# A four-layer attention block rewritten by chunks of 512 tokens, with the next key phase issued between attention steps

## The chip, the core and the metric

The kernel runs on one core of one Trainium2 chip. The metric is the device time in microseconds (us) of one execution. Engines are named as in the profile: PE (matrix engine), PEld (its weight loads), DVE (vector engine), ACT (scalar engine, which computes the exponentials), POOL (general-purpose engine), SP (the queue that issues DMA).

## The reference

A residual stream of 2048 tokens and 1024 features passes through four layers: A, B, A, B. All inputs are bf16. The same weights are used both times.

```python
def A(x, wqkv, w_phi, wo):          # linear attention, 32 heads of 32
    q, k, v = split(x @ wqkv)
    pq, pk = q @ w_phi, k @ w_phi   # per head
    phi_q = concat(softmax(pq), softmax(-pq));  phi_k = same of pk
    kv = phi_k^T v;  z = sum(phi_k)
    return (phi_q kv / (phi_q z + 1e-6)) @ wo

def B(x, wqkv, wo):                 # softmax attention, 32 heads of 32
    p = softmax(q k^T * 32**-0.5);  return (p v) @ wo

x = x + A(layernorm(x));  x = x + B(layernorm(x))   # twice
```

In layer B the exponentials are 32 heads x 2048 x 2048 numbers. ACT works on 128 rows at a time, so that is 1024 instructions of 128x1024 per layer, and 2048 in all, in both kernels.

## The kernel before

Each layer keeps everything in SBUF and runs in phases, one after the other: layer norm and projections, attention, output projection. The attention loop: one iteration holds 128 keys, 512 queries and 4 heads, so two exponentials of 128x1024.

```python
for ii, (g, qc, kc) in enumerate(iters):
    ...
    for pr in range(2):                       # two exponentials of this iteration
        e = epool.tile([P, 2 * C512], BF16, ...)
        nc.scalar.activation(out=e[:], in_=s_cur[pr][:], func=ACT.Exp)
        e_tiles.append(e)
    if ii + 1 < len(iters):                   # scores of the NEXT iteration
        s_next = [spool.tile([P, 2 * C512], F32, ...) for pr in range(2)]
        emit_scores(*iters[ii + 1], s_next)   # 4 row-tiled matmuls, 512 wide
    for j in range(4):                        # numerator of this iteration
        nc.tensor.matmul(out=num_ps[hsl, :], lhsT=v_aug[...], rhs=e_tiles[pr][...], ...)
    for j in range(4):                        # denominator of this iteration
        nc.tensor.matmul(out=den_ps[hsl, :], lhsT=ones_bf[:, 0:DH], rhs=e_tiles[pr][...], ...)
    ...                                       # (cut)
```

The softmax here doesn't subtract the row's maximum and nothing guards it: scores larger than these inputs give would overflow.

## Time and profile before

| | before |
|---|---|
| time, median of 2 runs | 3488.39 us (3488.2 to 3488.57) |
| mean granted PE clock | 0.973 |
| attention, start of the first exponential to end of the last, two layers | 938.8 + 938.9 us |
| everything else | 1606 us |
| exponentials, start to start inside attention | 0.904 to 0.917 us |

The first two lines below are from the page: busy time by engine, then the granted PE clock in tenths over 40 equal slices of the span. The page counts PE as busy while a matmul is anywhere in its pipeline, so 92% is not a peak.

```profile
PE 3190.9 (92%) x18316; PEld 1118.3 (32%) x18432; DVE 1359.2 (39%) x2009; ACT 2360.9 (68%) x2688; POOL 0.7 (0%) x6
...
PEclk9999989999999999999999988999999999999997
```

The window view sums busy time (and instruction counts) over stretches of the span. The second and fourth stretch are the two attention phases: ACT and PE are both filled, and DVE is nearly idle. The other three are everything else.

```profile
core 0: us, PE busy (x) PEld busy (x) DVE busy (x) ACT busy (x) POOL busy (x), PEclk, DMA share, GB/s
0.00:750.00 750.00, 590.57 (x2704) 258.19 (x2757) 516.81 (x848) 241.53 (x320) 0.70 (x6) 0.96 0.18 51
750.00:1688.00 938.00, 936.85 (x6136) 271.10 (x6132) 125.53 (x62) 937.88 (x1024) 0.00 (x0) 1.00 0.00 1
1688.00:2439.00 751.00, 643.91 (x2964) 279.12 (x3020) 542.35 (x875) 242.62 (x321) 0.00 (x0) 0.95 0.16 48
2439.00:3377.00 938.00, 936.83 (x6136) 271.12 (x6132) 125.53 (x62) 937.78 (x1024) 0.00 (x0) 1.00 0.00 1
3377.00:3484.00 107.00, 82.78 (x391) 38.75 (x391) 48.99 (x162) 1.07 (x2) 0.00 (x0) 0.79 0.17 59
```

The timeline lists instructions in order of start, with the duration in the second column. These are two half iterations in attention:

```profile
1000.53 0.39 PE L274 MATMUL spsn_7743<-qT,kT 32*128 32x512 bf16 x2
...
1000.85 0.39 PE L307 MATMUL num_ps<-E_7739,v_aug 128*32 128x512 bf16 x2
...
1001.02 1.29 ACT L295 ACTIVATE E_7757<-spsn_7743 128x1024 bf16<-128x1024 f32 x1
1001.08 0.38 PE L319 MATMUL den_ps<-E_7739,ones_bf 128*32 128x512 bf16 x1
...
1001.45 0.39 PE L274 MATMUL spsn_7744<-qT,kT 32*128 32x512 bf16 x2
...
1001.77 0.39 PE L307 MATMUL num_ps<-E_7741,v_aug 128*32 128x512 bf16 x2
...
1001.94 1.29 ACT L295 ACTIVATE E_7759<-spsn_7744 128x1024 bf16<-128x1024 f32 x1
```

ACT is the engine to watch: one 128x1024 exponential starts every 0.92 us (1001.02, 1001.94). It is recorded as 1.29 us long, so its record overlaps that of the next one; the first of a layer, with nothing in front of it, takes 1.02 us. So read the starts and not the durations. PE issues the scores of the next iteration (L274, `spsn`) as soon as a score tile is free, and does numerator (L307) and denominator (L319) while ACT works on the other tile. ACT never waits. Note that PE too is recorded as busy through the same 0.92 us; as these records include the pipeline, they do not show how much it could spare.

### The profile page before, as it was taken

To read this page: it belongs to the slowest core of one execution; us is meant where nothing else is said; L and a number is where in the kernel's file an instruction comes from. 1 tells how busy PE (TensorE), PEld (TensorE's weight loads), DVE (VectorE), ACT (ScalarE), POOL (GpSimd) and SP (SyncE) were. 2 spreads that over 40 slices of the span, in tenths; PEclk is the share of its full clock that TensorE was granted. 3 is DMA by queue.
4 is the path that set the end of the run, shared out by engine and by line. 5 is a ranking of instruction groups with operands and counts; after the bars stand their busy time and mean duration, and the time that the engine had idled before them with its cause. 6 is when DMAs were issued, how large, how long until landed. Compare 5 with 4: busy or idle time off the path is not lost.

```text
span 3483.5 us, 44252 instructions
## 1 busy us (share of the span) xinstructions
PE 3190.9 (92%) x18316; PEld 1118.3 (32%) x18432; DVE 1359.2 (39%) x2009; ACT 2360.9 (68%) x2688; POOL 0.7 (0%) x6
## 2 busy tenths in 40 slices
PE   2898679999999999999979976899999999999998
PEld 1343224432222222222334422344222222222223
DVE  2978876621111111111288888566011111111114
ACT  0125861039999999999312298100999999999970
POOL 0000000000000000000000000000000000000000
PEclk9999989999999999999999988999999999999997
DMA  6000001320000000000310000043000000000001
GB/s 132 15 1 1 1 25 61 128 78 1 1 1 1 1 1 1 1 1 1 74 49 1 1 1 0 25 145 121 1 1 1 1 1 1 1 1 1 1 25 49
DMA packets 112170, 82.67 MB, mean 24 GB/s; under 512 B 54624, under 2 KB 103776, under 8 KB 111968
## 3 DMA queue, kind: packets, MB, share of 16 engines
q1 hardware_dynamic: 111968, 79.84, 7.9%
q8 instruction: 144, 2.36, 0.3%
q14 instruction: 58, 0.48, 0.0%
HBM read 63.05 MB, written 4.19 MB: 19 GB/s over the span
## 4 chain that ended last, share of the span: by engine, by line
PE 75%; ACT 11%; DVE 10%; SPq 2%; issue 1%; DMA 1%; ACTq 0%; DVEq 0%
PE num_ps L307 19%; PE den_ps L319 13%; PE ps L167 7%; PE ps L222 6%; PE ps L245 3%; PE pkps L422 3%; ACT L548 2%; ACT L546 2%; DVE tmp L131 2%; ACT ebt L509 2%; DVE phik L449 1%; DVE xnT L134 1%; DVE ssum L445 1%; ACT e L441 1%; PE ps L142 1%
## 5 line engine op out<-in xcount | busy, mean ns | idle before, releaser
L330 DVE RECIPROCAL rden<-den_ps 128x512 f32<-128x512 f32 x64 | 214.9, 3358 | 1626.9 <-PE den_ps L319 1626.9
L274 PEld LDWEIGHTS <-kT 32*128 32x128 bf16 x4096 | 311.7, 91 | 872.8 <-issue 872.8
L307 PEld LDWEIGHTS <-v_aug 128*32 128x32 bf16 x4096 | 197.1, 93 | 465.6 <-issue 465.6
L222 PE MATMUL ps<-xnc,wslab 128*128 128x512 bf16 x1004 | 230.8, 386 | 15.2 <-DVE xnc L134 13.4
L167 PE MATMUL ps<-oT,wo_t 128*128 128x512 bf16 x1000 | 226.4, 386 | 16.2 <-DMA wo_t<-in_B_wo_dram 14.6
L422 PE MATMUL pkps<-W_pk,xnT 128*128 128x512 bf16 x994 | 239.2, 379 | 1.4
L441 ACT ACTIVATE e<-pkps 128x512 bf16<-128x512 f32 x128 | 76.2, 597 | 225.8 <-PE pkps L422 197.9
L117 ACT ACT_TABLE_LOAD x16 | 20.5, 1283 | 298.8 <-DVE t_386 L114 94.4
L319 PEld LDWEIGHTS <-ones_bf 128*32 128x32 bf16 x4096 | 208.8, 95 | 0.0
L491 PE MATMUL pqps<-xnT,W_pq 128*128 128x512 bf16 x496 | 160.7, 440 | 1.5 <-issue 0.7
L167 PEld LDWEIGHTS <-wo_t 128*128 128x128 bf16 x1024 | 101.7, 99 | 149.8 <-issue 33.9
L222 PEld LDWEIGHTS <-wslab 128*128 128x128 bf16 x1024 | 101.4, 99 | 142.8 <-issue 27.6
L142 PE MATMUL ps<-wv,xnT 128*128 128x512 bf16 x502 | 117.0, 380 | 21.6 <-DVE xnT L134 20.2
L174 DVE TENSOR_TENSOR xT<-xT,ps 128x512 bf16<-128x512 bf16 x128 | 87.4, 687 | 123.6 <-PE ps L167 121.7
L422 PEld LDWEIGHTS <-xnT 128*128 128x128 bf16 x1024 | 95.2, 98 | 91.6
L245 PE MATMUL ps<-wslab,xnc 128*128 128x512 bf16 x504 | 111.4, 379 | 0.4
L445 DVE TENSOR_REDUCE ssum<-e 128x16 f32<-128x512 bf16 x128 | 87.6, 685 | 39.6 <-ACT e L441 38.7
L449 DVE TENSOR_TENSOR phik<-e,rs 128x512 bf16<-128x512 bf16 x128 | 88.0, 691 | 11.8
L491 PEld LDWEIGHTS <-W_pq 128*128 128x128 bf16 x512 | 55.9, 110 | 92.0 <-issue 52.5
L546 ACT ACT_TABLE_LOAD x64 | 82.1, 1283 | 1.1
L548 ACT ACT_TABLE_LOAD x64 | 82.1, 1283 | 1.1
L509 ACT ACTIVATE ebt<-pqps 128x512 bf16<-128x512 f32 x128 | 74.5, 598 | 11.8 <-PE pqps L491 5.8
(9623 smaller groups left out, 7096.0 us busy)
## 6 DMA issues: line engine op xcount, KB each, us to landing
wslab<-in_B_wqkv_dram SPq DMA_DIRECT2D x48, 1024.0 KB, 5.0
wo_t<-in_A_wo_dram SPq DMA_DIRECT2D x2, 2048.0 KB, 9.7
wv<-in_A_wqkv_dram SPq DMA_DIRECT2D x2, 2048.0 KB, 7.9
wo_t<-in_B_wo_dram SPq DMA_DIRECT2D x2, 2048.0 KB, 8.8
out_dram<-tr SPq DMA_DIRECT2D x16, 256.0 KB, 2.0
phi<-in_A_w_phi_dram SPq DMA_DIRECT2D x64, 2.0 KB, 1.6
wqT<-in_A_wqkv_dram SPq DMA_TRANSPOSE x16, 4.2
wkT<-in_A_wqkv_dram SPq DMA_TRANSPOSE x16, 4.2
```

Source lines behind the costliest of these rows:

```text
L142: nc.tensor.matmul(ps[:], lhsT=xn_lhsT_fn(po), rhs=wv[:, po, fc * C512:(fc + 1) * C512], start=(po == 0), stop=(po == PO - 1),)
L167: nc.tensor.matmul(ps[:], lhsT=wo_t[:, po, ft * P:(ft + 1) * P], rhs=oT[:, po, cs], start=(po == 0), stop=(po == PO - 1),)
L222: nc.tensor.matmul(ps[:], lhsT=wt[:, po, gi * P:(gi + 1) * P], rhs=xnc[:, po, :], start=(po == 0), stop=(po == PO - 1),)
L245: nc.tensor.matmul(ps[:], lhsT=xnc[:, po, st * P:(st + 1) * P], rhs=wt[:, po, :], start=(po == 0), stop=(po == PO - 1),)
L274: nc.tensor.matmul(out=s_tiles[pr][:, jj * C512:(jj + 1) * C512], lhsT=kT[prt, g, k_sl], rhs=qT[prt, g, q_sl], start=True, stop=True, tile ...
L307: nc.tensor.matmul(out=num_ps[hsl, :], lhsT=v_aug[:, kc, g, j * DH:(j + 1) * DH], rhs=e_tiles[pr][:, jj * C512:(jj + 1) * C512], start=(kc ...
L319: nc.tensor.matmul(out=den_ps[hsl, :], lhsT=ones_bf[:, 0:DH], rhs=e_tiles[pr][:, jj * C512:(jj + 1) * C512], start=(kc == 0), stop=(kc == ...
L330: nc.vector.reciprocal(out=rden[:], in_=den_ps[:])
L422: nc.tensor.matmul(ps[:], lhsT=xnT[:, po, t * P:(t + 1) * P], rhs=W_pk[:, po, fc * C512:(fc + 1) * C512], start=(po == 0), stop=(po == PO ...
L491: nc.tensor.matmul(ps[:], lhsT=W_pq[:, po, g * P:(g + 1) * P], rhs=xnT[:, po, cs], start=(po == 0), stop=(po == PO - 1),)
L546: nc.scalar.activation(out=t3_list[gg][:], in_=t3_list[gg][:], func=ACT.Ln)
L548: nc.scalar.activation(out=t3_list[gg][:], in_=t3_list[gg][:], func=ACT.Exp, scale=-1.0)
```

## The change

The intent: do less work outside attention, and hide some of the rest inside attention, where DVE was nearly idle. The rewrite

- works through the layers by chunks of 512 tokens, with x, K, V and normalised activations kept in DRAM between phases;
- folds `w_phi` into the projection weights once instead of once per A layer, computes the key projection of layer A once instead of twice, and loads one ACT table for the whole kernel (before: 160 table loads of 1.28 us);
- applies the layer norm's scale to the projections' outputs, and squares on POOL;
- in attention uses steps of 256 keys x 256 queries (again two exponentials of 128x1024 per step), and three score tiles in PSUM instead of two;
- issues "background" work between attention steps: the next query projection, the output projection of the chunk before, and in the first B layer the next A layer's key phase.

The diff, cut to the attention loop (all the rest is cut; the kernels share almost no line):

```diff
+    def step(self, q, kv, g, half, kc, begin, end, ...):
+        n = 3 if mode[0] == "narrow" else 2          # score tiles
+        ...
+        for k in range(2):
+            for j in range(4):                       # 8 score matmuls, 256 wide
+                PE.matmul(tiles[j // 2][:, o:o + QH], lhsT=kv[rows, 0, ...], rhs=q[rows, ...],
+                          tile_position=(32 * j, 0), ...)
+        for i in range(2):                           # two exponentials
+            SC.activation(out=e[:], in_=tiles[i][:], func=ACT.Exp, scale=SCALE)
+        self.lag = (kv, g, half, kc, begin, end, acc, oT, first, last, es)
+
+    def finish(self):                                # numerator and denominator
+        kv, g, half, kc, begin, end, ... , es = self.lag
+        self.lag = None
+        ...                                          # 16 matmuls, 256 wide, column-tiled
+
+    def together(att, blocks, bg, steps, per=None):
+        for b in blocks:
+            for _ in b:                              # b calls step(), then yields
+                got = 0.0
+                while alive and got < per:           # background, 4 matmuls
+                    u, end = next(bg)
+                    ...
+                att.finish()
-            if ii + 1 < len(iters):
-                emit_scores(g2, qc2, kc2, s_next)
-            for j in range(4): ...                   # numerator, denominator
```

The name `lag` suggests that a step should be finished after the next one has begun. But `finish` is called before the block goes on to its next `step`, so it finishes the step just issued.

## The prediction

> **What bounds the kernel now.** In attention it is ScalarE. The timeline of one stretch inside attention shows the exponentials (128x1024, 2048 of them) starting 0.904 to 0.917 us apart, each 1.02 us when nothing is in front of it and 1.29 us when queued. Window sums give PE and ACT both near full from 750 to 1688 us and from 2439 to 3377 us: 937.5 us per layer, 1875 of 3488 us. Numerator and denominator matmuls of one tile run while ACT works on the other. The other 1613 us are projections (0.216 us per 128x512 matmul), DVE chains, table loads (205 us), layer norms.
>
> **What the change does.** Removed: folding twice, the second copy of the key projection (256 matmuls per layer, 55 us), all table loads, some DVE reciprocals. Added: K, V, activations through DRAM, squares on POOL, scaling of outputs by rstd. Moved: three quarters of the query and output projections and (layer 0) of the next linear layer's key phase are meant to hide under attention.
>
> **Where I expect it to fail.** The built program's order of PE instructions in attention is: 8 score matmuls (N=256), up to 4 background matmuls, 16 numerator/denominator matmuls of the *same* step, next scores. There is no lag of a step. The Trainium skill ("TensorE: Matmul & The Clock Gate", Part 2, step 1) says matmuls stay in program order, so scores of step n+1 stand behind a wait for both exponentials of step n. ACT then idles each step. Cost of one step (it does the work of two exponentials, today 1.83 us), from the trace: both exponentials 1.94 us (first two of the layer); release of PE 0.05; 3.5 groups of four column tiles at about 0.12 (half of 0.227 seen at N=512) 0.45; change of tiling 0.10 (0.319 between score and numerator pair minus 0.216); two score groups and their latency 0.40; release of ACT 0.10. Sum about 3.05 us.
>
> The clock: in this trace a 3.4 us window with matmuls streaming under about 0.37 of it is followed by a granted clock of 0.5, which ends only after a window above about 0.66 (the same page, Part 1, names such windows). Steps without background work stream about 0.27, so they should fall to 0.5 and take about 3.7 us. I count 330 steps with useful background and 694 without: 330x3.07 + 694x3.67 = 3560 us, plus about 100 us of stalls for DMA inside background work.
>
> Outside attention I add per chunk: layer norm 17 us (POOL square estimated 1.1 to 1.3 us from 2.6 cycles per element, "GPSIMD Engine Reference", 3.1; PE waits), linear query chunk about 115, linear key chunk 57: about 1250 us in all.
>
> **Prediction: 4850 us, range 4350 to 5300.** Faster by over 2%: 0.03; within 2%: 0.02; slower: 0.95. The loss is on the critical path: in attention ACT->PE->ACT is one chain.
>
> **What would show it.** Two exponentials start 0.92 apart, then about 1.1 to 1.8 us of ACT idle released by PE scores, every step; ACT busy share falls below 60%; mean granted clock falls well under 0.97; the chain of waits alternates ACT and PE in attention. Elsewhere: PE idle around layer norms, released by POOL and DVE.
>
> **What would make it wrong.** The clock staying full in sparse attention (then about 4400); four column tiles not running together, or weight loads not hidden at N=256 (above 5300); faster wide phases; or PE overtaking the waiting matmuls (then near 3200).

## The result

| | before | changed |
|---|---|---|
| time, median of 2 runs | 3488.39 us | 5198.38 us (5197.94 to 5198.81) |
| attention | 1878 us | 1776 + 1815 = 3591 us |
| everything else | 1606 us | 1606 us |
| mean granted PE clock | 0.973 | 0.681 |
| ACT busy share | 68% | 42% |

The ratio is 1.486, with a 95% interval of 1.470 to 1.503. A ratio is the mean time of one kernel's fast runs over that of the other's of the same rounds, so it is not quite the ratio of the medians quoted.

The whole loss, 1713 us, is in attention. Everything else takes what it took before in sum. The same two lines of the page after the change, then the same window view:

```profile
PE 3167.5 (61%) x29982; PEld 1346.2 (26%) x30208; DVE 1326.9 (26%) x1808; ACT 2160.7 (42%) x2353; POOL 276.9 (5%) x218
...
PEclk9777787755696588578557877855585567556555
```

```profile
core 0: us, PE busy (x) PEld busy (x) DVE busy (x) ACT busy (x) POOL busy (x), PEclk, DMA share, GB/s
0.00:928.00 928.00, 574.30 (x2326) 248.43 (x2371) 434.13 (x629) 94.68 (x161) 138.70 (x113) 0.81 0.37 117
928.00:2705.00 1777.00, 1088.11 (x13181) 465.79 (x13283) 344.21 (x408) 1021.31 (x1078) 69.08 (x54) 0.67 0.12 41
2705.00:3341.00 636.00, 425.88 (x1678) 175.64 (x1704) 298.58 (x396) 52.40 (x90) 69.15 (x51) 0.81 0.35 115
3341.00:5156.00 1815.00, 1054.54 (x12710) 446.33 (x12758) 234.52 (x333) 992.28 (x1024) 0.00 (x0) 0.58 0.09 29
5156.00:5197.00 41.00, 24.66 (x108) 9.98 (x98) 15.50 (x43) 0.00 (x0) 0.00 (x0) 0.71 0.07 26
```

In the attention stretches ACT is busy for 1021 of 1777 us and 992 of 1815 us; before, it was full. PE is busy for longer than before, but with gaps, and its clock is granted at 0.67 and 0.58.

The timeline of one step without background work (clock at half). The bracket gives the idle time of the engine before the instruction and what ended it:

```profile
1299.89 1.02 ACT L505 ACTIVATE E_7480<-s_7470 128x1024 bf16<-128x1024 f32 x1 [1.73 <-PE s_7471 L496]
...
1300.82 1.02 ACT L505 ACTIVATE E_7482<-s_7471 128x1024 bf16<-128x1024 f32 x1
1300.97 0.40 PE L527 MATMUL nd_7484<-E_7480,kv_6740 128*32 128x256 bf16 x2 [1.17 <-ACT E_7480 L505]
...
1301.88 0.40 PE L527 MATMUL nd_7484<-E_7482,kv_6740 128*32 128x256 bf16 x2 [0.52 <-ACT E_7482 L505]
...
1302.48 0.44 PE L527 MATMUL nd_7484<-E_7482,ones 128*32 128x256 bf16 x2
...
1302.85 0.40 PE L496 MATMUL s_7501<-q_2496,kv_6740 32*128 32x256 bf16 x2
...
1303.05 0.42 PE L496 MATMUL s_7502<-q_2496,kv_6740 32*128 32x256 bf16 x2
...
1303.56 1.02 ACT L505 ACTIVATE E_7511<-s_7501 128x1024 bf16<-128x1024 f32 x1 [1.73 <-PE s_7502 L496]
```

And a step with background work (`bg`, four matmuls, clock full):

```profile
1395.79 1.02 ACT L505 ACTIVATE E_8307<-s_8296 128x1024 bf16<-128x1024 f32 x1
...
1396.86 0.29 PE L527 MATMUL nd_8243<-E_8307,kv_8210 128*32 128x256 bf16 x2 [0.63 <-ACT E_8307 L505]
...
1397.40 0.28 PE L496 MATMUL s_8330<-q_4159,kv_8210 32*128 32x256 bf16 x2
...
1397.73 1.04 PE L156 MATMUL bg_8309<-c_1412_8230,w_8234 128*128 128x512 bf16 x4
1397.90 1.02 ACT L505 ACTIVATE E_8340<-s_8330 128x1024 bf16<-128x1024 f32 x1 [1.09 <-PE s_8331 L496]
```

Read ACT first. The two exponentials start 0.92 us apart, as before. Then ACT is idle for 1.73 us (half clock) or 1.09 us (full clock), each time released by PE's scores. Now read PE: the sixteen `nd` matmuls cannot go on until the second exponential has ended (1300.82 + 1.02 = 1301.84; PE starts at 1301.88), and the scores of the next step stand behind them. The scores needed nothing from this step: their inputs were long there, and a third score tile was free.

The step adds up from these lines. At full clock: exponentials 1.94 us, release of PE 0.05, numerator and denominator up to the scores 0.54, scores up to the next exponential 0.50: 3.03 us. At half clock: 1.95 + 0.04 + 0.97 + 0.71 = 3.67 us. The trace has 1022 intervals between steps inside the two layers: 280 are under 3.1 us, 717 between 3.60 and 3.75, and 25 others.

### The profile page after: what moved, and what is told of

Same layout as the page of the kernel before. It is cut to its first block, busy times and chain, and to the rows that moved or that the text cites. A ratio compares the mean times of both kernels' runs of the same rounds, so it can differ in the third digit from the quotient of the medians.

```text
span 5197.0 us, 68008 instructions
## 1 busy us (share of the span) xinstructions
PE 3167.5 (61%) x29982; PEld 1346.2 (26%) x30208; DVE 1326.9 (26%) x1808; ACT 2160.7 (42%) x2353; POOL 276.9 (5%) x218
## 4 chain that ended last, share of the span: by engine, by line
PE 45%; ACT 21%; issue 18%; DVE 7%; POOL 1%; DMA 0%; another core or an unknown queue 0%; ACTq 0%; POOLq 0%; DVEq 0%; SPq 0%
PE nd_7976 L527 0%; PE nd_28185 L527 0%; PE nd_36665 L527 0%; PE nd_12464 L527 0%; PE nd_39829 L527 0%; PE nd_40078 L527 0%; PE nd_26208 L527 0%; PE nd_6989 L527 0%; PE nd_40816 L527 0%; PE nd_20937 L527 0%; PE nd_19701 L527 0%; PE nd_15758 L527 0%; PE nd_39088 L527 0%; PE nd_38322 L527 0%; PE nd_36173 L527 0%
## 5 line engine op out<-in xcount | busy, mean ns | idle before, releaser
L527 PEld LDWEIGHTS <-ones 128*32 128x32 bf16 x8192 | 417.8, 118 | 24.7
L183 PEld LDWEIGHTS <-ones 128*128 128x128 bf16 x128 | 12.9, 103 | 168.6 <-issue 167.2
L379 PEld LDWEIGHTS <-Rsel 128*128 128x128 bf16 x128 | 17.0, 133 | 143.7 <-issue 143.7
L156 PEld LDWEIGHTS <-c_109_666 128*128 128x128 bf16 x128 | 14.0, 110 | 38.7 <-issue 28.5
L156 PEld LDWEIGHTS <-c_266_1434 128*128 128x128 bf16 x128 | 13.7, 107 | 36.4 <-issue 25.4
L156 PEld LDWEIGHTS <-c_34_316 128*128 128x128 bf16 x128 | 14.2, 111 | 34.2 <-issue 24.2
L156 PEld LDWEIGHTS <-c_3416_21758 128*128 128x128 bf16 x128 | 13.3, 104 | 32.9 <-issue 21.1
L156 PEld LDWEIGHTS <-c_188_1054 128*128 128x128 bf16 x128 | 13.1, 104 | 32.5 <-issue 20.2
```

The costliest lines, as they stand in the source:

```text
L156: PE.matmul(ps, lhsT=lhsT(po), rhs=rhs(po), start=(po == 0), stop=(po == G - 1))
L183: PE.matmul(ps, lhsT=ones_bf[:], rhs=sq[:], start=(po == 0), stop=(po == G - 1))
L379: PE.matmul(ps, lhsT=Rsel[:, g, s, :], rhs=ab[:], start=True, stop=True)
L527: PE.matmul(nd[rows, part * QH:(part + 1) * QH], lhsT=ones_bf[:, 0:32] if part else kv[:, 1, col:col + 32], rhs=es[j // 2][:, j % 2, i, :] ...
```

## The experiments

"On top of e1" means that the file starts from e1_lag. All results were correct. Each pair of numbers "attention / rest" is from the trace: start of the first to end of the last exponential of each layer, and what is left of the span.

### e1_lag: finish a step one step later

```diff
-            self.lag = (kv, g, half, kc, ..., es)
+            self.lag.append((kv, g, half, kc, ..., es))
-        def finish(self):
-            if self.lag is None:
+        def finish(self, keep=1):
+            if len(self.lag) <= keep:
                 return
-            kv, g, ... = self.lag
-            self.lag = None
+            kv, g, ... = self.lag.pop(0)
...
-                        if nxt is None and g + 1 < G:
+                        if nxt is None and g + 1 < G and (half or kc):   # load K, V once the old tile is free
...
                 att.finish()
+        att.finish(0)                                # at the end of a block
```

> Edit: numerator and denominator matmuls of a step are issued one step later, after the next step's scores; nothing else. Theory A (the order of PE instructions makes a step one chain of ACT and PE): ACT becomes the limit again, 1.83 to 2.1 us per step of two exponentials in place of 3.03 and 3.67, the two attention stretches together fall from 3591 us to 1900 to 2150, the whole to 3500 to 3750 us. Rival B (the 256-wide matmuls, twice as many weight loads and changes of tiling are what costs): PE stays the limit, steps stay above 2.6 us, the whole above 4500. Rival C (background work in between blocks PE): steps with background stay near 3 us, those without fall to 1.83, the whole about 3900.

Measured: 3617.88 us (4 runs, 3611.61 to 3619.29), against 3489.1 us of the kernel before; ratio 1.0365, interval 1.034 to 1.039. Attention 2007 / rest 1603 us. Of 1022 steps 978 are under 3.1 us, and the median is 1.833 us. A few lines give back 1584 us of attention; background work, matmul width, tiling and weight loads are as in the changed kernel. In the timeline the next scores now come between the finish of the last step and this one's first `nd` matmuls, and one bracket-less row of ACT merges six exponentials without a gap:

```profile
1048.73 5.93 ACT L505 ACTIVATE E<-s 128x1024 bf16<-128x1024 f32 x6
...
1050.67 0.76 PE L496 MATMUL s<-q,kv 32*128 32x256 bf16 x8
...
1051.37 0.29 PE L526 MATMUL nd<-E,kv 128*32 128x256 bf16 x2
...
1052.51 0.76 PE L496 MATMUL s<-q,kv 32*128 32x256 bf16 x8
```

Rivals B and C fall: the 256-wide matmuls fit, and steps with projections in the background take 2.04 us on average, not 3 (most take 1.81 to 1.87 us and one in eight 3.37; see e7).

### e2_pad: add useless matmuls

```diff
+                if got < 2:          # no background work in this step
+                    pad()            # 4 matmuls 128x128x512 into a PSUM tile that nobody reads
                 att.finish()         # order as in the changed kernel
```

> Edit: the changed kernel as it is, with four useless 128x128x512 matmuls put into every attention step that has no (or almost no) background matmuls; order unchanged. Theory A with the clock as its second term: those steps stream enough to keep the granted clock at full, every step takes about 3.03 us, attention falls from 3591 to about 3110 us and the whole from 5197 to 4650 to 4780 us, although work was added. Rival (the two step lengths come from the presence of background work in another way, or the clock is no cause): no change or slower, 5190 or more.

Measured (single look): 4779.47 us, 419 us less than the changed kernel, at the upper edge of what was expected. 969 of 1022 steps are now under 3.1 us with a median of 3.027 us. Attention 3172 / rest 1605 us. The granted clock in the two attention stretches (in each line the busy times are followed by the granted clock, then the DMA share and the GB/s) went from 0.67 and 0.58 to 0.97 and 0.99:

```profile
928.00:2517.00 1589.00, 1147.79 (x14432) 493.49 (x14435) 344.23 (x408) 1021.30 (x1078) 69.07 (x54) 0.97 0.14 46
3153.00:4737.00 1584.00, 1152.07 (x14418) 485.45 (x14414) 234.47 (x333) 992.07 (x1024) 0.00 (x0) 0.99 0.10 34
```

So the loss in attention has two terms, and they are told apart: the order makes 3.03 us of a 1.83 us step, and the emptiness that the order leaves on PE halves the clock, which makes 3.67 us of most of them.

### e3_ring2: two score tiles in place of three, order unchanged

```diff
-            n = 3 if mode[0] == "narrow" else 2
+            n = 2
```

> Edit: two score tiles in place of three in attention. Theory A: without a lag the third tile is never waited for, so no change, 5170 to 5225 us. Rival (score buffers limit the steps): over 2% slower.

Measured (single look): 5196.98 us. The third score tile is of no use in the changed kernel.

### e4_lag_ring2: the lag with two score tiles

> Edits: lag of one step as in e1_lag, but two score tiles in place of three. Theory A: the second half of the next scores must wait for the second exponential, ACT idles about 0.5 us at full clock and 0.75 at half, steps of 2.4 to 2.75 us, the whole 4050 to 4450 us; so lag and third tile are needed together. Rival (the lag alone is enough): equal to e1_lag.

The edit is that of e1_lag and e3_ring2 together. Measured (single look): 4199.41 us; median steps of 2.39 us at full and 2.50 us at half clock; attention 2591 / rest 1607 us. The lag alone is worth about 1000 us. With it the third tile is worth another 580 us, without it nothing (e3).

### e5_lag_nobg: on top of e1, no background work

```diff
-                while alive and got < per:
+                while False:
...
         att.finish(0)
+        set_mode("wide"); drain(bg); set_mode("narrow")   # the same work after the block
```

> Edit: on top of e1_lag, nothing is issued between attention steps; the same projections, key phase and output run after each attention block instead. If the interleaving does what it was meant for (hide that work), attention falls to 1024 steps of 1.81 to 1.83 us, 1875 us, and the work taken out comes back in full, some 480 us: the whole 3880 to 4060 us. Rival (interleaving costs attention as much as it hides): 3618 or less.

Measured (single look): 3995.95 us. Steps have a median of 1.833 us in every block. So the interleaving does hide work, 378 us of it net, once the order is right.

### e6_lag_sqact: on top of e1, squares of the layer norm on ACT outside attention

```diff
-            (DVE if fast and po % 2 else POOL).tensor_tensor(out=sq[:], in0=xc[...], in1=xc[...], op=ALU.mult)
+            if mode[0] == "wide":
+                SC.activation(out=sq[:], in_=xc[:, po, :], func=ACT.Square)
+            else:
+                POOL.tensor_tensor(...)
```

> Edit: on top of e1_lag, the squares of the layer norm outside attention run on ACT in place of POOL. If outside attention PE waits for POOL's squares (1.41 us each, eight per layer norm, and DVE's centring slowed to 1.31 us beside them), each of 13 layer norms gets about 5 us shorter: the part outside attention 1603 to about 1535, the whole 3530 to 3575 us. Rival (the next link, DVE's centring, is as long anyway): 3600 or more.

Measured: 3540.45 us (2 runs). Attention 2015 / rest 1526 us: 77 us less, 5.9 us for each of 13 layer norms outside attention. In the changed kernel one layer norm reads like this (timeline; the first row merges eight centring instructions of DVE, and PE waits for each square of POOL):

```profile
471.99 9.96 DVE L173 TENSOR_TENSOR c_448_2282<-x_1966,f_2280 128x512 bf16<-128x512 bf16 x8
472.83 1.36 POOL L179 TENSOR_TENSOR sq_2284<-c_448_2282 128x512 bf16<-128x512 bf16 x1 [80.33 <-DVE c_448_2282 L173]
...
474.24 0.59 PE L183 MATMUL wide_2271<-sq_2284,ones 128*128 128x512 bf16 x1 [3.01 <-POOL sq_2284 L179]
...
```

With the squares on ACT the same two chains are (timeline of e6_lag_sqact):

```profile
446.49 4.90 DVE L173 TENSOR_TENSOR c<-x,f 128x512 bf16<-128x512 bf16 x8
447.21 4.90 ACT L180 ACTIVATE sq<-c 128x512 bf16<-128x512 bf16 x8 [56.66 <-DVE c L173]
```

Eight centring instructions took 9.96 us beside POOL and take 4.90 us beside ACT.

### e7_lag_fine: on top of e1, three background matmuls per step, squares issued ahead

```diff
-            if po == 3:
-                yield 4, False
+            if po < G - 1:
+                yield 1, False
...
-  chain(*work), 128, per=4)
+  chain(*work), 128, per=3)
```

(and in the layer norm, in attention only, one pause between the squares and the matmuls that read them)

> Edit: on top of e1_lag, three background matmuls per attention step in place of four, and in attention the layer norm's squares are issued one slot ahead of the matmuls that read them. If the 132 us that e1_lag's attention is above 1875 us come from steps in which four background matmuls make PE the limit (2.04 us) and from PE standing behind the squares, attention falls to 1890 to 1950 us, the whole to 3500 to 3565 us. Rival (contention with the background on ACT or DMA): 3600 or more.

Measured: 3574.26 us (2 runs), attention 1968 / rest 1604 us. The direction is right and the size is missed: 39 us of the 132 came back, where 57 or more were expected. The longest step went from 10.2 to 5.0 us. The two traces also show that part of the reason was wrong. The 2.04 us of a step with projections in e1_lag is a mean: four background matmuls fit into 1.81 to 1.87 us, but one step in eight takes 3.37. In the one that begins at 945.69 us PE waits 1.46 us for DVE's copy of a background tile (`q`), which stands in DVE's queue behind the reciprocal of 1.75 us that ends an attention half. In e7_lag_fine these steps take 1.81 to 1.83 us, but about one in 24 takes 3.06. Some steps with the key phase in the background take about 2.85 us. In these (19 in e7_lag_fine) ACT also does the key phase's two exponentials of 128x512 and has no idle time over 0.15 us: the time is ACT's own work. What holds the others, up to 4.97 us, was not tested.

### e9_sqact_exps: on top of e6, the key phase's exponentials straight from PSUM

```diff
-                pk = T("f", [P, C], F32)
-                DVE.tensor_scalar(out=pk[:], in0=ps, scalar1=rcol[:, t:t + 1], ..., op0=ALU.mult)
...
-                        out=e[:, s, :], in_=pk[:], func=ACT.Exp, scale=1.0 - 2.0 * s
+                        out=e[:, s, :], in_=ps, func=ACT.Exp, scale=(res["ncol"] if s else rcol)[:, t:t + 1]
```

> Edit: on top of e6_lag_sqact, the exponentials of the key phase read PSUM directly, with the row scale as their own scale, so DVE's copy (0.69 us) drops out of each of its 64 units per layer. If the key phase outside attention is limited by DVE (about 3.2 us per unit against 1.73 us of PE), its 40 units there save about 0.7 us each: 3500 to 3520 us, attention a little shorter too. Rival (PE or POOL limits it): 3535 to 3545, as e6_lag_sqact.

(The kernel has 8 such units per chunk, so 32 per layer and not 64; the 40 outside attention are right. The edit also adds a negated row scale, `ncol`, and two more buffers for small tiles.)

Measured (single look): 3465.2 us, attention 2006 / rest 1457 us. The saving is 75 us, more than twice what was expected, so my reason was not the whole. One unit of the key phase in the changed kernel shows why:

```profile
183.16 0.74 DVE L249 TENSOR_SCALAR f_883<-wide_874,sm_708 128x512 f32<-128x512 f32 x1
183.96 3.57 PE L156 MATMUL wide_874<-w_754,c_109_666 128*128 128x512 bf16 x8 [6.00 <-DVE f_883 L249]
...
184.00 1.15 ACT L254 ACTIVATE ea_885<-f_883 128x512 bf16<-128x512 f32 x2 [3.19 <-DVE f_883 L249]
...
185.25 1.22 DVE L258 TENSOR_REDUCE sm_888<-ea_885 128x32 f32<-128x1024 bf16 x1 [1.34 <-ACT ea_885 L254]
...
186.50 0.35 DVE L262 RECIPROCAL sm_890<-sm_888 128x32 f32<-128x32 f32 x1
...
187.57 0.75 DVE L249 TENSOR_SCALAR f_902<-wide_874,sm_708 128x512 f32<-128x512 f32 x1
```

From one copy (L249, 183.16) to the next (187.57) are 4.41 us, not the 3.2 us of DVE's work. DVE's instructions stand in the order of the program here: the sum (L258) waits 1.34 us for ACT's exponentials, which wait for the copy, and the copy of the next unit stands behind the sum. It is the fault of the attention loop once more, in small. In e9_sqact_exps ACT starts from PSUM, DVE's chain has nothing that waits for itself, and a unit takes 2.31 us (L260 to L260):

```profile
153.67 1.21 DVE L260 TENSOR_REDUCE sm<-ea 128x32 f32<-128x1024 bf16 x1
...
154.98 0.35 DVE L264 RECIPROCAL sm<-sm 128x32 f32<-128x32 f32 x1
...
155.98 1.21 DVE L260 TENSOR_REDUCE sm<-ea 128x32 f32<-128x1024 bf16 x1
```

### e10_sqact_otact: on top of e6, two DVE jobs of the query phase on ACT

```diff
-        DVE.reciprocal(out=t1[q0, :], in_=t1[q0, :])
+        SC.activation(out=t1[q0, :], in_=t1[q0, :], func=ACT.Ln)
+        SC.activation(out=t1[q0, :], in_=t1[q0, :], func=ACT.Exp, scale=-1.0)
...
-            DVE.tensor_copy(out=oT[:, g, :], in_=ps)
+            SC.copy(out=oT[:, g, :], in_=ps)
```

> Edit: on top of e6_lag_sqact, in the query phase the eight output copies per chunk and the reciprocal of 32x512 go from DVE to ACT. If PE waits there for DVE (reciprocal 3.4 us in a chain of 10 us; 24 copies and products of 0.6 us for 16.6 us), eight chunks save 5 to 7 us each: 3480 to 3505 us. Rival: 3535 to 3545.

Measured (single look): 3505.41 us, attention 2012 / rest 1491 us: 35 us, 4.4 us per chunk, a little under what was expected. In the changed kernel PE is idle for 10.12 us in each of eight chunks while DVE works through eleven small instructions, one reciprocal of 3.34 us among them:

```profile
420.06 3.34 DVE L365 RECIPROCAL f_2106<-f_2106 32x512 f32<-32x512 f32 x1
...
427.20 0.59 PE L379 MATMUL wide_2088<-ab_2108,Rsel 128*128 128x512 bf16 x1 [10.12 <-DVE ab_2108 L371]
```

### e8_all: e1 with e6, e7, e9, e10 and a second PSUM bank for the last transposes

The edits are those above; in attention the layer norm's squares run on DVE; the 32 transposes at the end alternate between two banks.

> Edit: e1_lag with e6 and e7 together, squares in attention on DVE, exponentials of the key phase straight from PSUM, two DVE jobs of the query phase (output copies, one reciprocal) on ACT, and two PSUM banks for the last transposes. Worked out from the idle times of e1_lag's profile: attention about 1900, the rest 1603 less 65 (squares), 30 (key phase), 50 (query phase), 10 (end): 3300 to 3420 us, which would be faster than the kernel before by 2 to 5%. If it is not below 3420, one of these links was not the one waited for.

Measured: 3375.64 us (4 runs, 3374.12 to 3376.72), against 3486.33 us of the kernel before; ratio 0.9684, interval 0.9668 to 0.9701. Attention 1962 / rest 1411 us. This version beats both kernels, the one before by 3.2%.

### e11_before_serial: the same fault put into the kernel before

```diff
-                        if ii + 1 < len(iters):
-                            ...
-                            emit_scores(g2, qc2, kc2, s_next)
                         for j in range(4): ...       # numerator
                         for j in range(4): ...       # denominator
+                        if ii + 1 < len(iters):
+                            ...
+                            emit_scores(g2, qc2, kc2, s_next)
```

> Edit: the kernel before, with the next scores issued behind the numerator and denominator matmuls in place of ahead of them; the built order shows it half by half (numerator, denominator, next scores of one tile, then of the other). Theory A by the same sums: from the end of one exponential 0.05, two groups 0.43, tiling change 0.1, scores and latency 0.40, release 0.1, then 1.02 of exponential, 2.1 us for a loop that holds two exponentials: 2.1 to 2.2 us per pair in place of 1.83, so plus 280 to 380 us, 3760 to 3880 us; much less than the 1.2 to 1.8 us per pair of the changed kernel, because one tile's work still covers the other's. Rival (the order does not matter for the kernel before): 3490.

Measured: a fast run of 3770.54 us and a slow one of 3890.48 us, against 3487.45 us of the kernel before. Only the slow run was traced. In it, where the clock was full, a pair of exponentials takes 2.107 us; 1024 of those and the 1605 us of the rest make 3763 us, which is within 0.2% of the fast run. So the order costs about 283 us there, by one fast run. That it costs less than in the changed kernel I put down to the scheduled order, which goes half by half: while one tile's chain runs, ACT still has the other tile. The changed kernel's finish waits for both tiles at once. This comparison is read from the order and was not tested by itself. Part of the second layer of the slow run was at half clock with 3.02 us per pair; nothing is concluded from that.

## Why the prediction was right

Point by point:

1. **The order of PE instructions makes a step one chain.** Right. The prediction took from the Trainium skill, "TensorE: Matmul & The Clock Gate", Part 2, step 1, that matmuls stay in program order and only weight loads are pulled ahead. The trace agrees: in the steps shown no score matmul starts before the last `nd` matmul of the step before, although the third tile was free (e3: 5196.98 us without it). e1 shows that the order alone carries the loss from a 1.83 us step to 3.03 us.
2. **Cost of a step at full clock, 3.05 us.** Measured 3.03. Term by term: exponentials 1.94 (1.94), release of PE 0.05 (0.05), numerator, denominator and tiling change 0.55 (0.54), scores to ACT 0.50 (0.50). All came from durations in the trace of before. The change of tiling is 0.10 us as predicted: from the last `nd` group to the first scores there are 0.21 to 0.22 us, and 0.107 of it is the group itself.
3. **The clock.** Right. Steps without background work were predicted at half clock and 3.67 us; measured 3.67, and e2 shows the cause by adding matmuls and gaining 419 us. I had counted 330 steps at full and 694 at half clock; the trace has 280 and 717, with 25 others.
4. **Attention in all.** Predicted 3560 + 100 for DMA stalls in the background; measured 3591. The stalls were mis-sized: only 18 intervals are over 3.75 us, and their excess over 3.67 is 21 us.
5. **Outside attention, "about 1250 us in all".** This is the term that was mis-sized: measured 1606 us. The layer norm was about right (17 us predicted; PE waits from 471 to 488 us in the one shown). A key chunk took 78 to 85 us from one layer norm to the next where 57 were predicted: I summed DVE's work and did not see that DVE and ACT wait for each other there (4.41 us per unit; e9). A query chunk took 128.5 us where 115 were predicted. That is about 115 us for five key chunks and 108 us for eight query chunks. The remaining 130 us or so, by subtraction, are the start, the second fold of weights, the extra query projections and the end, for which my sum held about 45 us.
6. **The sum itself.** 3560 + 100 + 1250 are 4910 us; the text said 4850. The measured 5198 us lies 288 us above the sum of the terms, and in the stated range, 102 us below its upper end. Attention was 69 us too high and the outside 356 us too low, a miss that the width of the range took up.

Where the expected gain went is thus answered in two parts. In attention, hiding can work (e5, with the order put right: 378 us) but was buried under the chain. Outside, PE's work did shrink (busy 1317 us before, 1025 us after, from the window views), but the time was turned into waits: PE for POOL's squares (77 us, e6), DVE and ACT for each other (69 us of the rest, e9), PE for DVE (35 us, e10). DMA, an obvious suspect with x, K and V now in DRAM, does not show as the cause: PE's idle gaps of over 0.15 us outside attention add up to about 270 us before and 573 us after, and those that DMA ended to 77 and 31 us. The granted clock outside attention fell as well, from 0.95 or 0.96 in the two long stretches to 0.81; what that cost by itself was not tested. With the lag alone the kernel is still 3.7% slower than before; with those waits taken out as well it is 3.2% faster.

## What to carry to other kernels

In an in-order engine queue, look for an instruction whose inputs are ready but which stands behind one that waits for another engine: issue the next step's independent work first, and give it a buffer of its own, since the lag was worth 1000 us with two score tiles and 1580 us with three, while the third tile without the lag was worth nothing. Check the built order of each queue and not the name of a variable, and look for the same chain in the small loops too (DVE and ACT in the key phase). A gap on PE can cost twice: here the sparse PE was granted a clock of 0.67 and 0.58 in attention. Whether that is so can be tested with useless matmuls (e2).

## What the Trainium skill lacked or had wrong

- "TensorE: Matmul & The Clock Gate", Part 1, "HAM oscillation — how this bites in real kernels", puts the rule as no PE-idle gaps over about 3.4 us. In the changed kernel the clock went to half at 979 us, when the background work of the first block had run out, and stayed there until 1392 us, with no gap between matmuls over 1.2 us in the steps around the drop. What goes with it is the share of a 3.41 us window in which matmuls stream (each recorded duration less 0.165 us, the 0.38 us record of a 128x512 matmul less the 0.216 us from start to start, then merged): in the traces of before and after, every window at full clock that was followed by half clock was at or under 0.39, and every one at half clock that was followed by full clock was at or over 0.66. The converse does not hold: after the change, windows of as little as 0.36 stayed at full clock and windows of up to 0.91 stayed at half; and in e8_all one of 0.51 was followed by half clock. So this is what goes with the clock in two traces and not a threshold. The page gives no such shares.
- "TensorEngine Tiling (Array Packing)", "Key Properties", says that a change of tiling mode drains the engine, without a cost. Here it was 0.10 us at full clock and about 0.16 us at half (0.37 us from the last `nd` group to the scores, less the 0.214 us from one `nd` group to the next), at the change from `nd` to scores.
- "GPSIMD Engine Reference", section 1, names contention with VectorE instructions that have two SBUF inputs, and no page that I found gives a time for this pair of instructions. Here DVE's centring of 128x512 took 1.31 us on average beside POOL's squares, and eight of them 9.96 us against 4.90 us beside ACT's (e6). A POOL square took 1.41 us on average, where 512 elements at the 2.6 cycles of section 3.1 would be 1.1 us, an estimate; but the last square of the layer norm shown, when DVE's centring was over, took 1.03 us, so that the page's figure fits and the rest goes with DVE's work beside it.
- "VectorE: DVE Perf Modes" has no time for a reciprocal. Here 128x512 in f32 took 3.36 us, 128x256 1.75 us, and 32x512 3.34 us: 32 rows took as long as 128.
